# Attention's steps two by two in an order given to TensorE, beside the first feed-forward

## The chip, the cores and the metric

The program runs on one core of a Trainium2 chip. The metric is the device time of one execution in microseconds (us). The engines that matter are TensorE (PE, matrix multiplication, with its weight loads shown apart as PEld), VectorE (DVE), ScalarE (ACT), GpSimd (POOL), and SyncE (SP), which issues most of the DMAs. Each engine works through its own instructions in the order in which they stand in the program, and waits where a result of another engine is missing.

## The reference

Three layers follow each other. Attention has 4 batches of 8 heads, 576 positions and 64 columns to a head; its result is mixed with a read of a memory. Two feed-forward layers with 2304 tokens, 512 columns and 2048 hidden columns follow.

```python
scores = scale * np.matmul(q, k.transpose(0, 1, 3, 2))     # causal mask, softmax
local = np.matmul(a, v)
mem_ret = np.einsum('bhsd,bhde->bhse', q_p, M_prev)        # q_p = phi(q)
mem_out = mem_ret / mem_norm
attn = g * mem_out + (1 - g) * local
h = x @ w_in;  g = h * np.cos(h);            x = g @ w_out  # first feed-forward
h = x @ w_in;  g = h * np.tanh(softplus(h)); y = g @ w_out  # second feed-forward
```

## The kernel before

**Attention.** Two heads go together as a pair, 16 pairs in all. The queries of a pair are cut into five pieces, i = 0 to 4, of 128 positions; the last has 64 positions, and its two heads share one piece. One (pair, piece) is a step, so there are 80 steps, numbered from 0. A step has three stages, all in `attention`:

- Stage a (L240) multiplies queries with keys into PSUM (`sp`, L253: one matmul for each head with 64 contraction rows, so that the two heads use the upper and the lower half of the array; L266 for the last piece, with all 128 rows). VectorE adds the mask and finds the row's extreme (L255, L268), ScalarE takes the exponential and its sum (L258, L273), VectorE the reciprocal (L278), and GpSimd scales the rows (`at`, L280). With piece 0 the memory's read of the pair is made (`memory`, L284: `mp`, L293).
- Stage b (L304) transposes the rows `at` on TensorE, 128 columns at a time (`tp`, L313; `td`, L319, for the last 64 keys), and ScalarE and VectorE copy them to SBUF in turn (`aT`, `aD`).
- Stage c (L324) adds in one PSUM tile `o` the memory's share (L329, a matmul with the identity over all 128 output rows) and, for each 128 keys, the product with V of each head (L340, 64 output rows each, so that the two heads use the left and the right half of the array; the last 64 keys with 64 contraction rows too). ScalarE and VectorE then split the result into `xH` and `xL`, and SyncE stores them.

The text calls a matmul that uses the whole array full shape, the one of L253 half rows, the one of L340 half columns. Every float32 matmul of attention other than a transposition stands in the profile as two passes. The two heads of a half-row or half-column pair run at the same time when they stand next to each other.

**First feed-forward.** It runs over blocks of 256 tokens. One unit of `first` (L416) makes 24 matmuls into `h` (L429), and one unit of `second` (L436) makes 24 into `y` (L495). The cosine between them (`elem_cos`, L374) uses ScalarE (`u`, L383, and the sine, L388, with a table load before it and another one before the next exponential), VectorE and GpSimd (`g`, L401). A block of tokens can begin when its batch has left attention.

**What sets the order.** The loop at L354 issues for each s the stages c of step s-4, b of s-2 and a of s (LAGC, LAGB). The driver (L873 to L895) takes each yield: on "a" it issues conversions of weights, on "c" as many units of the first feed-forward as a target allows (L890 to L895). A scheduler in the framework then places the instructions on each engine by its own estimate of time, so feed-forward matmuls are put between those of attention wherever that estimate has room. `tc.issue_after(x)` adds only an order: the instructions in its block stand behind x on x's engine.

Of the kernel before, what the change touches and what calls it, by code (L numbers as in the profile page):

```python
# [23 lines left out]
RES = 2  # L24
# [10 lines left out]
PACE1 = 1.5  # L35
# [16 lines left out]
def attention_moe_moe_kernel(  # L52
# [140 lines left out]
    def attention(ap, pools):  # L193
# [46 lines left out]
        def stage_a(b, p, i):  # L240
            if i == 0:
                memory(b, p)
# [5 lines left out]
            if i < 4:  # L248
                N = P * (i + 1)
                sps = [bank("S", [P, SM], "sp") for _ in range(2)]  # L250
                for j, sp in enumerate(sps):
                    rows = slice(j * D, (j + 1) * D)
                    nc.tensor.matmul(sp[:, :N], st["q"][rows, q0:q0 + P], st["k"][rows, :N], start=True, stop=True)  # L253
# [7 lines left out]
            else:  # L261
                N = S
                at = ats[0]
                for k0, k1, w, name in ((0, SM, SM, "sp"), (SM, S, D, "sd")):
                    out = bank("S", [P, SM], name)
                    nc.tensor.matmul(out[:, :w], st["q"][:, q0:q0 + P], st["k"][:, k0:k1], start=True, stop=True)  # L266
# [17 lines left out]
        def memory(b, p):  # L284
# [3 lines left out]
            for c0, c1 in ((0, 3), (3, NQ)):  # L288
                nb = c1 - c0
                mp = bank("T", [P, nb, P + 2], "mp")  # L290
                for c in range(c0, c1):
                    q0 = min(c * P, S - P)
                    nc.tensor.matmul(mp[:, c - c0], st["ph"][:, q0:q0 + P], st["mz"], start=True, stop=True)  # L293
# [10 lines left out]
        def stage_b(b, p, i):  # L304
# [3 lines left out]
            for at in st["at", i]:  # L308
# [15 lines left out]
        def stage_c(b, p, i):  # L324
# [4 lines left out]
            nc.tensor.matmul(o[:, :n], st["mo"][:, i], ident[:, P - n:], start=True, stop=False,  # L329
                             skip_group_check=True)  # L330
            for c in range(i + 1):
                kk = P if c < 4 else D
                for j in range(2):
                    if i < 4:
# [17 lines left out]
        ns = len(steps)  # L352
        prep(*pairs[0])
        for s in range(ns + LAGC):  # L354
            if 0 <= s - LAGC < ns:
                stage_c(*steps[s - LAGC])
                yield "c", s - LAGC
            if 0 <= s - LAGB < ns:
                stage_b(*steps[s - LAGB])
                yield "b", s - LAGB  # L360
            if s < ns:
                b, p, i = steps[s]
                if i == PREP:
                    nx = s // NQ + 1
                    if nx < len(pairs):
                        prep(*pairs[nx])
                stage_a(b, p, i)
                yield "a", s
# [638 lines left out]
```

## Time and profile before

| | |
|---|---|
| median of 3 runs | 1042.88 us (1040.84 to 1043.91) |
| profiled execution | 1043.82 us, its span 1042.0 us |
| PE busy | 1006.5 us (97%), 6704 matmuls |
| DVE / POOL / ACT busy | 681.8 / 618.5 / 576.6 us |
| mean granted TensorE clock | 0.99 |
| chain that ended last | PE 65%, DVE 9%, DMA 8%, POOL 7%, issue 6% |

A row of the timeline gives the start, how long it lasted, engine, line, operation, the tiles (out<-in), the shape and how many instructions are merged. Matmuls overlap: the time that a group takes from the others is from its start to the start of the next row, not its own length. Attention's last matmul starts at 383.9 us, and the first matmul of the first feed-forward at 119.5 us; between those two both layers share TensorE.

### The profile page before, as it was taken

To read this page: it belongs to the slowest core of one execution; us is meant where nothing else is said; L and a number is where in the kernel's file an instruction comes from. 1 tells how busy PE (TensorE), PEld (TensorE's weight loads), DVE (VectorE), ACT (ScalarE), POOL (GpSimd) and SP (SyncE) were. 2 spreads that over 40 slices of the span, in tenths; PEclk is the share of its full clock that TensorE was granted. 3 is DMA by queue.
4 is the path that set the end of the run, shared out by engine and by line. 5 is a ranking of instruction groups with operands and counts; after the bars stand their busy time and mean duration, and the time that the engine had idled before them with its cause. 6 is when DMAs were issued, how large, how long until landed. Compare 5 with 4: busy or idle time off the path is not lost.

```text
span 1042.0 us, 19347 instructions
## 1 busy us (share of the span) xinstructions
PE 1006.5 (97%) x6704; PEld 895.9 (86%) x6704; DVE 681.8 (65%) x1423; ACT 576.6 (55%) x1274; POOL 618.5 (59%) x600
## 2 busy tenths in 40 slices
PE   6988999999999999999999999999999999999996
PEld 3755787787878899998788887899999999999996
DVE  4689865657665545777756776258787447862557
ACT  5886676758575643334546565347554545445441
POOL 3379744455553524665755776246877768786661
PEclk8998999999999999999999999999999999999999
DMA  7477734556442337433678777998988888798772
GB/s 268 143 237 237 224 112 161 184 177 213 138 148 82 139 106 261 154 108 126 223 269 280 281 291 289 399 311 291 385 295 272 273 284 288 244 297 267 262 239 107
DMA packets 121841, 236.19 MB, mean 227 GB/s; under 512 B 11920, under 2 KB 35984, under 8 KB 121744
## 3 DMA queue, kind: packets, MB, share of 16 engines
q1 hardware_dynamic: 117136, 220.27, 62.8%
q10 hardware_dynamic: 4608, 14.68, 3.5%
q8 instruction: 54, 0.88, 0.3%
q14 instruction: 43, 0.35, 0.1%
HBM read 176.44 MB, written 58.46 MB: 225 GB/s over the span
## 4 chain that ended last, share of the span: by engine, by line
PE 65%; DVE 9%; DMA 8%; POOL 7%; issue 6%; ACT 4%; SPq 1%; DVEq 0%; ACTq 0%; POOLq 0%
PE h L779 14%; PE y L750 13%; PE h L429 12%; PE y L495 11%; PE o L340 5%; PE tp L313 3%; PE sp L253 3%; PE o L329 2%; DVE wst L148 1%; DMA woD<-ws 1%; DVE wst L147 1%; POOL g L401 1%; DMA w<-woD 1%; PE mp L293 1%; DMA wst<-in_w1o_dram 1%
## 5 line engine op out<-in xcount | busy, mean ns | idle before, releaser
L684 POOL TENSOR_TENSOR g<-us,g 128x384 fp32r<-128x384 f32 x164 | 182.5, 1129 | 92.9 <-ACT g L131 92.7
L495 PE MATMUL y<-g,w 128*128 128x256 f32 (+1 forms) x1344 | 221.8, 318 | 3.2 <-ACT aT L131 1.6
L495 PEld LDWEIGHTS y<-g,w 128*128 128x128 f32 x1344 | 191.6, 190 | 30.7 <-issue 10.5
L429 PE MATMUL h<-xbH,w 128*128 128x256 f32 (+1 forms) x896 | 206.1, 317 | 1.4 <-DMA xbH<-xsH 1.3
L750 PE MATMUL y<-g,w 128*128 128x384 f32 x1008 | 194.7, 335 | 2.0 <-POOL g L684 1.4
L779 PE MATMUL h<-xc,wq 128*128 128x384 f32 x1008 | 194.8, 335 | 0.9 <-DVE us L673 0.9
L750 PEld LDWEIGHTS y<-g,w 128*128 128x128 f32 x1008 | 176.0, 188 | 4.1 <-POOL g L684 2.3
L401 POOL TENSOR_TENSOR g<-u,g 128x512 fp32r<-128x512 f32 x72 | 105.9, 1485 | 122.3 <-ACT g L131 40.1
L779 PEld LDWEIGHTS h<-xc,wq 128*128 128x128 f32 x1008 | 176.1, 188 | 1.2 <-DVE us L673 1.2
L280 POOL TENSOR_SCALAR at<-at,sm,omg 128x128 f32<-128x128 f32 (+2 forms) x144 | 112.9, 793 | 104.6 <-DVE sm L278 86.3
L429 PEld LDWEIGHTS h<-xbH,w 128*128 128x128 f32 x896 | 151.1, 191 | 14.0 <-DMA xbH<-xsH 1.8
L429 PE MATMUL h<-xbL,w 128*128 128x256 f32 (+1 forms) x448 | 140.8, 315 | 0.6 <-DMA xbL<-xsL 0.6
L673 DVE TENSOR_TENSOR us<-h,us 128x384 f32<-128x384 f32 x120 | 66.2, 553 | 91.2 <-PE h L779 76.2
L131 ACT ACTIVATE g<-us 128x384 fp32r<-128x384 f32 x168 | 85.7, 523 | 52.7 <-DVE us L668 28.5
L383 ACT ACTIVATE u<-h 128x512 int32<-128x512 f32 x72 | 42.8, 594 | 95.9 <-PE h L429 85.5
L429 PEld LDWEIGHTS h<-xbL,w 128*128 128x128 f32 x448 | 85.6, 191 | 6.2 <-DMA xbL<-xsL 1.1
L677 ACT ACTIVATE us<-us 128x384 f32<-128x384 f32 x72 | 37.7, 525 | 91.8 <-DVE us L673 86.7
L258 ACT ACTIVATE at<-at,mn 128x128 f32<-128x128 f32 (+3 forms) x128 | 71.1, 557 | 26.9 <-DVE mn L255 24.4
L384 DVE SCALAR_TENSOR_TENSOR u<-u,h 128x512 f32<-128x512 int32 x72 | 48.9, 681 | 47.5 <-ACT u L383 44.5
L148 DVE SCALAR_TENSOR_TENSOR wst<-wst 128x512 int32<-128x512 int32 x64 | 75.4, 1187 | 0.4
L714 DVE TENSOR_TENSOR ac<-y,ac 128x384 f32<-128x384 f32 x120 | 63.8, 550 | 18.0 <-PE y L750 17.1
L340 PE MATMUL o<-aT,vt 128*64 128x128 f32 (+1 forms) x896 | 67.3, 275 | 2.6 <-ACT aT L131 2.6
(109 smaller groups left out, 1519.7 us busy)
## 6 DMA issues: line engine op xcount, KB each, us to landing
wq<-wsD SPq DMA_DIRECT2D x168, 256.0 KB, 4.5
w<-woD SPq DMA_DIRECT2D x168, 256.0 KB, 4.5
wsD<-ws SPq DMA_DIRECT2D x18, 512.0 KB, 3.5
woD<-ws ACTq DMA_DIRECT2D x18, 512.0 KB, 5.3
wst<-in_w1i_dram SPq DMA_DIRECT2D x16, 512.0 KB, 4.1
wst<-in_w1o_dram SPq DMA_DIRECT2D x16, 512.0 KB, 4.6
wst<-in_w2i_dram SPq DMA_DIRECT2D x16, 512.0 KB, 4.2
wst<-in_w2o_dram SPq DMA_DIRECT2D x16, 512.0 KB, 5.4
```

Source lines behind the costliest of these rows:

```text
L131: eng.activation(dst, src, AF.Copy, scale=scale)
L148: nc.vector.scalar_tensor_tensor(lo, hi, 3, lo, ALU.logical_shift_left, ALU.bitwise_or)
L258: marks["act"] = nc.scalar.activation(at[:, :N], at[:, :N], AF.Exp, bias=mn[:, j:j + 1], scale=-1.0, accum_out=sm[:, j:j + 1]).ins
L280: marks["pool"] = turn_of("sc", b == 0).tensor_scalar(at[:, :N], at[:, :N], sm[:, j:j + 1], gates[j], ALU.mult, ALU.mult).ins
L340: marks["pe"] = nc.tensor.matmul(o[j * D:(j + 1) * D, :n], st["vt"][:kk, c, j * D:(j + 1) * D], a, start=False, stop=c == i, skip_group_ch ...
L401: marks["gl"] = turn_of(kind).tensor_tensor(gL, g, gH.bitcast(F32), ALU.subtract).ins
L429: nc.tensor.matmul(h[:, a * T:(a + 1) * T], w_[:, c, f0:f0 + P], x_[c], start=m == 0, stop=m == 3 * NC - 1)
L495: nc.tensor.matmul(y[e // per][:, cols], w_[:, f, es], g_, start=fst and m == 0 and e % per == 0, stop=lst and m == 2, skip_group_check=True)
L673: marks['v'] = nc.vector.tensor_tensor(c, b, x, ALU.add).ins
L684: ins = turn_of("ml" if k + 1 < n else "mz").tensor_tensor(t[:, 1], x, t[:, 0].bitcast(F32), ALU.subtract).ins
L750: nc.tensor.matmul(y, w_[:, wl, c], x[:, xl], start=m == 0, stop=m == 3 * KS - 1, skip_group_check=True)
L779: nc.tensor.matmul(b, w[name][:, wl, c], x[name][:, xl, c], start=first and m == 0, stop=m == 5, skip_group_check=True)
```

## The change

From step 30 on (PAIRS) the loop goes two steps at a time. Each stage of the two steps is issued behind the last matmul issued so far (`marks["pe"]`), so TensorE's order is given: the stages c that are due, then one or two units of the first feed-forward (PACE), then the memory's read, the stages b, and the stages a, the longer of the two first. Stage b lags a by one turn for the even step and by two for the odd one. The memory's share becomes two matmuls of 64 output rows. The last 64 keys of V are laid into the lower half of 128 rows, the upper half zero, and the transposition of the last keys takes 128 columns of `at`; so the last product has 128 contraction rows.

```diff
-RES = 2
-PACE1 = 1.5
+PAIRS = 30
+PACE = (1, 2, 2, 1, 2)
...
                 for c in range(0, W, P):
-                    nc.tensor.transpose(tp[:, c:c + P], at[:, c:c + P], ident)
+                    marks["pe"] = nc.tensor.transpose(tp[:, c:c + P], at[:, c:c + P], ident).ins
...
-                aD = ap.tile([P, 2, D], F32, tag="aD", name="aD", bufs=BUFS["aD"])
+                aD = ap.tile([P, P], F32, tag="aD", name="aD", bufs=BUFS["aD"])
                 tp = bank("T", [P, SM], "td")
-                nc.tensor.transpose(tp[:D, :P], at[:, SM:], ident)
-                scaled("aD", aD.rearrange("p a b -> p (a b)")[:D, :P], tp[:D, :P])
+                marks["pe"] = nc.tensor.transpose(tp[:, :P], at[:, S - P:], ident).ins
+                scaled("aD", aD, tp[:, :P])
...
-            nc.tensor.matmul(o[:, :n], st["mo"][:, i], ident[:, P - n:], start=True, stop=False,
-                             skip_group_check=True)
+            for j in range(2):
+                rows = slice(j * D, (j + 1) * D)
+                nc.tensor.matmul(o[rows, :n], st["mo"][:, i, rows], ident[:, P - n:], start=True, stop=False,
+                                 skip_group_check=True)
...
-                        a = st["aT", i][1][:D, j]
+                        a = st["aT", i][1][:, rows]
                     marks["pe"] = nc.tensor.matmul(
-                        o[j * D:(j + 1) * D, :n], st["vt"][:kk, c, j * D:(j + 1) * D], a,
+                        o[rows, :n], st["vt"][:, c, rows], a,
                         start=False, stop=c == i, skip_group_check=True).ins
...
+        def run(stage, ss):
+            for s in ss:
+                if 0 <= s < ns:
+                    with tc.issue_after(marks["pe"]):
+                        stage(*steps[s])
...
+        for s in range(PAIRS, ns + LAGC + 1, 2):
+            both = (s, s + 1)
+            run(stage_c, upto(s - LAGC + 1, 0))
+            yield "c", s - LAGC
+            for k in both:
+                coming(k)
+            run(banked, both)
+            run(stage_b, upto(s - LAGB + 1, 1))
+            run(stage_a, sorted(both, key=lambda k: -(k < ns and steps[k][2])))
+            for k in both:
+                if k < ns:
+                    yield "a", k
...
-        share = (r + 1) / steps_b
-        tgt = int(2 * NTL * (b - 1 + (share ** PACE1 if b == 1 else share))) - RES
-        while k_done < tgt:
-            converted(4 * min(k_done + 2, NTL))
-            _, kk = next(m1)
-            k_done = max(k_done, kk + 1)
+        stored[0] = (s + 1) // steps_b
+        for _ in range(PACE[s // 2 % NQ] if s >= PAIRS - LAGC else 0):
+            converted(4 * min(k_done // 4 * 2 + 3, NTL))
+            with tc.issue_after(marks["pe"]):
+                next(m1)
+            k_done += 1
...
     def rows(x):
         t = np.zeros((B, H, NQ * 128, D), x.dtype)
-        t[:, :, :S] = x
+        t[:, :, :S - D] = x[:, :, :S - D]
+        t[:, :, S:] = x[:, :, S - D:]
```

Before, TensorE's order puts the scores of one step, head by head, between matmuls of the feed-forward. L253 is the score matmul, L313 the transposition and L495 the feed-forward's `y`:

```order
L313 MATMUL tp<-ident,at 128x128 x4
L253 MATMUL sp<-kd,qd 128x512
L495 MATMUL y<-g,w_100 128x256 x2
L495 MATMUL y<-g,w_101 128x256
L495 MATMUL y<-g,w_100 128x256 x2
L253 MATMUL sp<-kd,qd 128x512
L495 MATMUL y<-g,w_101 128x256
```

The two heads' scores are five feed-forward matmuls apart, each with a change of shape before and behind it.

Now the order of the two steps 48 and 49 stands as follows, from the end of a feed-forward unit (h, L461) to the start of the next (y, L527). L314 is the transposition, L265 and L251 are the scores of the last piece and of the others, L332 the memory's share and L343 the product with V:

```order
L461 MATMUL h_2841<-xbH_1521,w011_95 128x256
L314 MATMUL tp_2893<-ident_73,at_2617 128x128
L314 MATMUL tp_2897<-ident_73,at_2618 128x128
L314 MATMUL tp_2901<-ident_73,at_2759 128x128 x2
L314 MATMUL tp_2906<-ident_73,at_2760 128x128 x2
L265 MATMUL sp_2914<-kd_2425,qd_2427 128x512
L265 MATMUL sd_2917<-kd_2425,qd_2427 128x64
L251 MATMUL sp_2928<-kd_2425,qd_2427 128x512
L251 MATMUL sp_2929<-kd_2425,qd_2427 128x512
L332 MATMUL o_2948<-ident_73,mo_2564 64x128 x2
L343 MATMUL o_2948<-aT_2894,vt_2431 64x128
```

The scores of both steps and the products with V now stand together, without feed-forward matmuls between them; 24 `y` matmuls, the memory's read and six transpositions follow, and then `tp_3016`, the transposition of the rows whose scores are `sp_2928`.

On ScalarE the piece of the order before one of the copies that stage c needs (`aT_2591`, of step 42; L415 and L420 are the feed-forward's `u` and its sine, L232 and L233 prepare the queries of a later pair) is now:

```order
L415 ACTIVATE u_2422<-h_2524 128x512
L347 ACTIVATE xH_2162<-o_2517 128x128
L232 ACTIVATE ph_3170<-qt_3168 128x576
L131 ACTIVATE aT_2581<-tp_2580 128x256
L420 ACT_TABLE_LOAD
L420 ACTIVATE u_2422<-u_2422,c_hpi_80 128x1024
L233 ACT_TABLE_LOAD
L233 ACTIVATE ph_3170<-ph_3170 128x576
L131 ACTIVATE aT_2591<-tp_2590 128x384
```

TensorE's matmuls behind `tp_2590` and `tp_2596` are the scores of steps 44 and 45 and then stage c of steps 41 and 42, whose last part begins with `aT_2591`; no feed-forward unit stands between.

## Rows read from the trace of the kernel before

**Rows 1.** Two stretches of 26 us: busy time of each engine, granted clock, DMA
```profile
core 0: us, PE busy (x) PEld busy (x) DVE busy (x) ACT busy (x) POOL busy (x), PEclk, DMA share, GB/s
104.00:130.00 26.00, 24.18 (x208) 18.68 (x208) 22.66 (x72) 18.06 (x58) 18.84 (x22) 0.93 0.69 221
...
260.00:286.00 26.00, 26.00 (x226) 22.73 (x227) 15.82 (x47) 14.21 (x42) 14.04 (x16) 1.00 0.42 137
```

**Rows 2.** Chain that ended last, 380 to 500 us: start, length, what
```profile
383.23 0.88 PE o L340 x20
...
391.61 5.76 PE h L429 x48
```

**Rows 3.** Timeline of PE, 268 to 280 us: start, length, engine, line, tiles, count
```profile
268.89 0.39 PE L329 MATMUL o<-ident,mo 128*128 128x128 f32 x2
269.21 0.88 PE L340 MATMUL o<-aT,vt 128*64 128x128 f32 x12
270.01 0.39 PE L429 MATMUL h<-xbH,w 128*128 128x256 f32 x1
270.24 0.28 PE L429 MATMUL h<-xbL,w 128*128 128x256 f32 x1
...
272.98 0.60 PE L313 MATMUL tp<-ident,at 128*128 128x128 f32 x4
273.41 0.27 PE L319 MATMUL td<-ident,at 128*64 128x128 f32 x1
273.61 0.70 PE L253 MATMUL sp<-kd,qd 64*128 64x256 f32 x4
274.25 0.49 PE L329 MATMUL o<-ident,mo 128*128 128x128 f32 x2
274.66 1.10 PE L340 MATMUL o<-aT,vt 128*64 128x128 f32 x16
275.69 0.74 PE L495 MATMUL y<-g,w 128*128 128x256 f32 x4
...
277.77 0.91 PE L253 MATMUL sp<-kd,qd 64*128 64x384 f32 x2
278.61 0.38 PE L495 MATMUL y<-g,w 128*128 128x256 f32 x1
```

**Rows 4.** Timeline of PE: three pauses, in brackets with what ended them
```profile
100.61 0.80 PE L329 MATMUL o<-ident,mo 128*128 128x128 f32 x2 [3.70 <-DVE mo L298]
...
117.09 0.49 PE L329 MATMUL o<-ident,mo 128*128 128x128 f32 x2 [1.82 <-DVE mn L255]
...
316.90 0.50 PE L495 MATMUL y<-g,w 128*128 128x256 f32 x2 [1.63 <-ACT aT L131]
```

**Rows 5.** Stretches behind the last two pauses, columns as in rows 1
```profile
117.60:120.90 3.30, 3.30 (x23) 2.97 (x24) 3.30 (x13) 1.73 (x7) 3.08 (x4) 0.50 0.52 158
...
318.70:322.10 3.40, 3.40 (x31) 3.40 (x30) 1.53 (x4) 2.58 (x9) 3.06 (x4) 1.00 0.34 130
```

**Rows 6.** Timeline of PE, from a feed-forward unit's end to the scores of step 48
```profile
201.41 0.60 PE L313 MATMUL tp<-ident,at 128*128 128x128 f32 x4
201.94 1.13 PE L253 MATMUL sp<-kd,qd 64*128 64x512 f32 x4
203.00 0.49 PE L329 MATMUL o<-ident,mo 128*128 128x128 f32 x2
```

**Rows 7.** Timeline of ACT, the same stretch
```profile
201.61 0.60 ACT L383 ACTIVATE u<-h 128x512 int32<-128x512 f32 x1 [1.44 <-PE h L429]
...
202.51 1.28 ACT L388 ACT_TABLE_LOAD   x1
203.80 1.15 ACT L388 ACTIVATE u<-u,c_hpi 128x1024 f32<-128x1024 f32 x1
...
206.26 0.72 ACT L258 ACTIVATE at<-at,mn 128x512 f32<-128x512 f32 x1
...
208.36 0.47 ACT L131 ACTIVATE aT<-tp 128x384 f32<-128x384 f32 x1
```

**Rows 8.** Timeline of POOL, the rows of step 48 scaled
```profile
211.01 1.51 POOL L280 TENSOR_SCALAR at<-at,sm,omg 128x512 f32<-128x512 f32 x2
```

**Rows 9.** Timeline of SP's queue: the first blocks' loads
```profile
89.31 1.00 SPq L482 DMA_DIRECT2D xbH<-xsH  x2
...
93.17 2.04 SPq L482 DMA_DIRECT2D xbL<-xsL  x2
```

**Rows 10.** Timeline of PE: step 27's stage c, the first feed-forward's first matmul
```profile
111.69 0.39 PE L329 MATMUL o<-ident,mo 128*128 128x128 f32 x2
...
119.53 0.56 PE L429 MATMUL h<-xbH,w 128*128 128x256 f32 x1
```

More of the change, by code (lines that the diff above doesn't have):

```diff
@@ L252, in stage_a @@
                     rows = slice(j * D, (j + 1) * D)
-                    nc.tensor.matmul(sp[:, :N], st["q"][rows, q0:q0 + P], st["k"][rows, :N], start=True, stop=True)
+                    marks["pe"] = nc.tensor.matmul(sp[:, :N], st["q"][rows, q0:q0 + P], st["k"][rows, :N],
+                                                   start=True, stop=True).ins
                 for j, (at, sp) in enumerate(zip(ats, sps)):
@@ L265, in stage_a @@
                     out = bank("S", [P, SM], name)
-                    nc.tensor.matmul(out[:, :w], st["q"][:, q0:q0 + P], st["k"][:, k0:k1], start=True, stop=True)
+                    marks["pe"] = nc.tensor.matmul(out[:, :w], st["q"][:, q0:q0 + P], st["k"][:, k0:k1],
+                                                   start=True, stop=True).ins
                     if k0 == 0:
@@ L292, in memory @@
                     q0 = min(c * P, S - P)
-                    nc.tensor.matmul(mp[:, c - c0], st["ph"][:, q0:q0 + P], st["mz"], start=True, stop=True)
+                    marks["pe"] = nc.tensor.matmul(mp[:, c - c0], st["ph"][:, q0:q0 + P], st["mz"],
+                                                   start=True, stop=True).ins
                 den = ap.tile([P, nb, 2], F32, tag="den", name="den", bufs=BUFS["den"])
@@ L352, in attention, with coming, banked, upto @@
         ns = len(steps)
+        def coming(s):
+            if s < ns and steps[s][2] == PREP and s // NQ + 1 < len(pairs):
+                prep(*pairs[s // NQ + 1])
+        def run(stage, ss):
[3 more added lines that the diff above has]
+                        stage(*steps[s])
+        def banked(b, p, i):
+            if i == 0:
+                memory(b, p)
         prep(*pairs[0])
-        for s in range(ns + LAGC):
-            if 0 <= s - LAGC < ns:
+        for s in range(PAIRS):
+            if s >= LAGC:
                 stage_c(*steps[s - LAGC])
                 yield "c", s - LAGC
-            if 0 <= s - LAGB < ns:
+            if s >= LAGB:
                 stage_b(*steps[s - LAGB])
[L360 to L368, printed above, removed]
+            coming(s)
+            banked(*steps[s])
+            stage_a(*steps[s])
+            yield "a", s
+        done = [PAIRS - LAGC, PAIRS - LAGB]
+        def upto(n, k):
+            out = range(done[k], n)
+            done[k] = n
+            return out
+        for s in range(PAIRS, ns + LAGC + 1, 2):
[10 more added lines that the diff above has]
+                    yield "a", k
     last_sin = [None]
@@ L494, in mm2_t @@
             for m, (w_, g_) in enumerate(((woH, gH), (woH, gL), (woL, gH))):
-                nc.tensor.matmul(y[e // per][:, cols], w_[:, f, es], g_, start=fst and m == 0 and e % per == 0,
-                                 stop=lst and m == 2, skip_group_check=True)
+                marks["pe"] = nc.tensor.matmul(y[e // per][:, cols], w_[:, f, es], g_,
+                                               start=fst and m == 0 and e % per == 0,
+                                               stop=lst and m == 2, skip_group_check=True).ins
     def part(ys_, blk, i):
```

13 lines of the change are left out of this document (3 added, 10 removed).

## The prediction

> **What bounds the kernel now.** I read the page's shares first, then the chain of waits, then a table by stretches, then TensorE's own timeline, and last the timelines of ScalarE and GpSimd at the places where TensorE will have to wait for them. The shares show TensorE busy for 97% of the span, and the chain gives it 65%. The table by stretches [rows 1] shows how this comes about inside attention: from 260 us TensorE is busy for the whole 26 us while VectorE, ScalarE and GpSimd stand at 14 to 16 us; from 104 us it has 24.18 of 26 us, with VectorE at 22.66 close behind. So behind step 23's stage c (100.61 us, behind the last long pause of the early part) TensorE's own work and its pauses set the pace, up to attention's last matmuls, which begin at 383.23 us and end at 384.1 [rows 2]. What follows is dense: 48 matmuls of the feed-forward in 5.76 us [rows 2], 0.12 us each, and nothing of the change lies there. What the change is worth is therefore TensorE's time saved between 100.6 and 384.1 us, less new pauses, and less what the clock takes.
>
> **Split heads.** I went along TensorE's order from stage c of step 23 to the end of the first feed-forward, before and after. Before, in ten steps the scores of the two heads stand apart (four of 384 columns, three of 512, two of 128, one of 256); after, in none. What standing apart costs is in TensorE's timeline [rows 3]: one head alone with 384 columns takes 0.84 us (277.77 to 278.61). Two heads with 256 columns take 0.64 (273.61 to 274.25), and two with 512 take 1.06 (201.94 to 203.00) [rows 6]. By these two, 384 columns for both would be between 0.64 and 1.06, 0.85, what one head alone takes. So a head alone costs as much as the pair, and each split step pays its pair's time once too often: 4 x 0.84 + 3 x 1.06 + 0.64 + 2 x 0.42 (an estimate, half of 0.84) = 7.9 us, about 8.0.
>
> **Changes of shape.** Along the same way the order has 213 changes between full, half-row and half-column shapes before and 88 after, 125 fewer. The price comes from TensorE's timeline [rows 3]. Full to half columns and back: the two passes of L329 take 0.32 (268.89 to 269.21) ahead of a change where two transpositions take 0.22, 0.10 more; the 12 passes of L340 take 0.80 where six pairs at 0.115 (the 16 passes at 274.66 take 1.03, so two more pairs 0.23) make 0.69, 0.11 more, or 0.14 by pairs at 0.11; the first h behind them takes 0.23 where a dense one takes 0.12, 0.11 more. Together 0.32 to 0.35; I take 0.35. Half rows: td, ahead of the change, takes 0.20 instead of 0.11, 0.09 more, and L329 between half rows and half columns (274.25 to 274.66) takes 0.41 instead of 0.32, again 0.09; I take 0.19 for both and the rounding. So one change costs 0.175 or 0.095. Between 125 x 0.095 = 11.9 and 125 x 0.175 = 21.9 us I take the middle, 16.9. The memory's share is no longer a full matmul: two half-column matmuls side by side cost a pair's two passes, 0.23, against 0.22, so nothing but the change of shape is saved, and that is counted.
>
> **V's last keys.** The last product has 128 instead of 64 contraction rows at the same columns, and the transposition td 128 instead of 64 output rows. The timeline [rows 3] has four transpositions from 272.98 to 273.41, 0.11 each, and td from 273.41 to 273.61, 0.20 with the change to half rows behind it. I put nothing for either, bounded by 0.1 us a last piece (ten of them, 1 us) both ways. The Trainium skill (TensorEngine Tiling (Array Packing), Key Properties) says that a change of tiling mode drains TensorE, and td with its 64 output rows would be such a change, in and out; by that rule ten of them at 0.135 twice would give 2.7 us more. The 0.43 us of the four rows ahead of td show no drain, so the trace does not bear it out there.
>
> So TensorE's work falls by 8.0 + 16.9 = 25 us, 20 to 30 by the bounds.
>
> **New pauses.** Before, matmuls of the feed-forward go wherever a step waits. Now the order is given, and the work behind a wait can't step ahead. I take two places of the ten steps after which pieces and PACE repeat; attention has five such tens from step 30.
>
> The first is the transposition tp_3016, which waits for the scaled rows of step 48. Before, from the unit's end (201.41) [rows 6] the path of scores, minimum, exponential [rows 7], scaling [rows 8] needed until 211.77 for the first head (211.01 and half of 1.51): 10.36 us; for the second 11.1. After, TensorE has between the two events: six transpositions 0.66, the scores of both steps 2.2 (1.06 for step 48, for the whole rows of step 49's piece an estimate of as much), ten pairs of half columns 1.15 with 0.24 for the changes, 24 y at 0.12 with a change 3.0, the memory's ten passes 1.1, six more transpositions 0.66; 9.0 us. The pause is 10.36 - 9.0 = 1.35 for the first head; the second head's rows come 0.74 later but are wanted only 0.44 later (four transpositions), 0.3 more: 1.65. It is 2.4 if one more exponential (0.72) [rows 7] stands ahead, since step 49's scores now go first. I take 2.0.
>
> The second is stage c of step 42, whose aT_2591 now stands on ScalarE behind u, a table load, the sine, another load and the two ph. Before, from the start of u to the first exponential behind the sine it took 4.65 (201.61 to 206.26), and a copy 0.47 [rows 7]. With two activations of the exponential's size for ph, 1.44, and 0.2 to the start of u, aT is there 6.8 us behind the start. TensorE has in that time the memory's read 1.1, transpositions 1.1, scores 1.06 and 0.93, changes and the first pairs 0.6; 4.8 us. Pause: 2.0.
>
> With some 1.1 us in small pauses a ten (from none, where the other wait is late enough, to twice that), this makes 5.1 us, five times 25.5. Bounds: 12.8, where half of each wait is covered by work that I counted as late, and 35. What goes are two pauses of before [rows 4], 1.82 (VectorE's minimum) and 1.63 (ScalarE's copy): 3.5 us. The pause of 3.70 lies ahead of the change.
>
> **The clock.** Behind the pause of 1.82 the granted clock was 0.50 for 3.3 us, 1.2 instead of 2.4 GHz; behind that of 1.63 it stayed at 1.00 [rows 5]. A fall costs half of its 3.4 us, 1.7. Ten pauses of about 2.0 come, one of two such was followed by a fall; since the fall stands in the stretch with the idler TensorE, 0.93 granted against 1.00 [rows 1], I take four of ten. One of before goes: 3 x 1.7 = 5.1 us more. Bounds: -1.7 and 9 x 1.7 = 15.3.
>
> **The sum** is made on the profiled execution, 1043.82 us (span 1042.0, the rest before and behind it unchanged): -25 + 25.5 - 3.5 + 5.1 = +2.1, so 1045.9. The profiled execution lies 0.9 above the median of the three runs; against the median the forecast is 1045.0. Little is changed for other queues: SP's and POOL's instructions keep nearly their sequence. The first unit comes right behind stage c of step 27, which before begins at 111.69 us, so some 7 us earlier than its 119.53 [rows 10]; its loads are issued from 89 to 95 us [rows 9], ahead of that. Were they late there, the unit would wait for what its earlier start gains and no more. With 44 units inside attention instead of 40, fewer dense matmuls follow; that is in the 25 us, as the count goes to the end of the first feed-forward.
>
> **Rivals.** *The clock falls behind every long pause, and TensorE is slower than before.* Mechanism: tp_3016 waits on GpSimd and aT_2591 on ScalarE at every ten, and half speed follows each time; ten falls at 1.7 in place of the one of before, 15.3 instead of 5.1, so +12.3: 1055. For it: every idle time in the order is a true one now. Against it: the pause of 1.63. It decides from the seventh fall on.
>
> *The waits are mostly covered.* The path of 10.36 us was measured where VectorE and ScalarE worked between other steps; if the new order brings the exponential and the scaling forward by 1 us, both pauses halve: 12.8 us, and with none followed by a fall, -25 + 12.8 - 3.5 - 1.7 = -17.4: 1025.5. For it: outside the stretch from 104 us the three engines have over 10 of 26 us idle [rows 1]. Against it: the order is strict.
>
> *VectorE becomes the bound from 104 us.* It is busy for 22.66 of 26 us [rows 1]; going 9% faster (25 of 283 us) it would be at 24.7, so any bunching makes it late, and a fifth of the 25 us, 5.0, is lost there: 1050.
>
> *A table load holds ScalarE for longer where a copy stands right behind it.* If each of the two loads ahead of aT_2591 held ScalarE for twice its 1.29 us (202.51 to 203.80) [rows 7], in five tens 2 x 1.29 x 5 = 12.9 us come on top: 1057.9. Against it: the sine starts right at the load's end, and the second load is already in the 4.65 us. The Trainium skill (ScalarE: Activation LUTs, What ACT_TABLE_LOAD costs) would have it so: about 1283 ns for the load and a drain of about 1380 ns, 2.66 us in all; the row of 1.29 shows the load and no drain.
>
> **How the numbers follow.** This kernel's measurement tells 0.3%, 3.1 us, from no change: 1039.8 to 1046.0. My forecast has 0.42 with its own range from 1037 to 1052 (shape changes 5 either way, pauses as much); 0.55 of it lies within 0.3%, a quarter below, a fifth above. The covered waits have 0.30, the clock 0.22, VectorE 0.03, the loads 0.03. Faster: 0.30 + 0.11 = 0.41. Same: 0.23. Slower: 0.22 + 0.03 + 0.03 + 0.08 = 0.36. The range goes from 1023 to 1058.
>
> **What would show it.** Each step right: scores of both heads as one row of four passes throughout; half-column rows that begin with the memory's share; pauses of about 2 us in TensorE's timeline at stage b, ended by GpSimd's scaling, and at stage c, ended by ScalarE's aT, two in ten steps; stretches at half clock behind some of them; the second feed-forward's first matmul some 2 us later than before. The forecast is wrong if the sum of TensorE's pauses in attention is under 13 us or over 35, if the clock never falls behind 104 us or falls at every ten, or if a pair of heads side by side takes more than here.

## The result and the profile after

The changed kernel takes 1058.48 us (median of 4 runs, 1056.42 to 1060.03) against 1043.39 us before; the ratio is 1.0146 with an interval of 1.0124 to 1.0169. It is slower, by 15 us where 2 were forecast, and lies half a microsecond above the upper end of the range. The profiled execution has a span of 1058.2 us, 16.2 more than before.

The page of the changed kernel, busy time by engine and the chain's shares:

```profile
span 1058.2 us, 19552 instructions
...
PE 997.1 (94%) x6864; PEld 897.7 (85%) x6864; DVE 683.2 (65%) x1423; ACT 578.1 (55%) x1276; POOL 617.9 (58%) x600
...
PE 54%; POOL 12%; DVE 11%; issue 8%; ACT 8%; DMA 5%; SPq 0%; ACTq 0%; DVEq 0%; POOLq 0%
```

TensorE was busy 97% of the time and is now at 94%; the chain passes from it to GpSimd, ScalarE and VectorE, so it waits for them. Where the time went is shown by two stretches of each kernel, the first from stage c of step 23 to the second half of the first feed-forward (its first matmul with 512 columns), the second from there to the end (columns as in [rows 1]). Before:

```profile
100.60:472.10 371.50, 366.88 (x3066) 316.47 (x3067) 240.75 (x642) 218.98 (x515) 185.55 (x200) 0.99 0.48 159
472.10:1042.00 569.90, 556.89 (x3026) 521.96 (x3024) 370.17 (x535) 280.38 (x528) 371.46 (x320) 1.00 0.79 272
```

After:

```profile
100.10:481.00 380.90, 354.28 (x3183) 317.35 (x3182) 239.09 (x642) 221.93 (x522) 186.92 (x199) 0.96 0.45 155
481.00:1058.20 577.20, 557.96 (x3026) 523.81 (x3024) 376.90 (x541) 282.01 (x531) 375.67 (x325) 0.99 0.78 270
```

The first stretch is 9.4 us longer, the second 7.3, though nothing of the change lies in the second. In the first, the mean granted clock falls from 0.99 to 0.96.

TensorE's pauses in the first stretch (its timeline; in brackets the pause and what ended it) are where the prediction had put them:

```profile
169.66 0.66 PE L314 MATMUL tp<-ident,at 128*128 128x128 f32 x4 [1.78 <-POOL at L280]
171.58 0.63 PE L314 MATMUL tp<-ident,at 128*128 128x128 f32 x4 [1.27 <-POOL sw L595]
...
196.58 0.44 PE L332 MATMUL o<-ident,mo 128*64 128x128 f32 x4 [1.79 <-ACT aT L131]
...
225.28 0.66 PE L314 MATMUL tp<-ident,at 128*128 128x128 f32 x4 [1.79 <-POOL at L280]
226.48 0.63 PE L314 MATMUL tp<-ident,at 128*128 128x128 f32 x4 [0.55 <-DVE mo L299]
227.04 1.65 PE L251 MATMUL sp<-kd,qd 64*128 64x256 f32 x8
...
306.62 0.44 PE L332 MATMUL o<-ident,mo 128*64 128x128 f32 x4 [1.84 <-ACT aT L131]
```

225.28 is tp_3016, the transposition of step 48, with 1.79 us where 2.0 were taken; 196.58 is stage c of step 42, 1.79 where 2.0 were taken. ScalarE's timeline ahead of it shows the chain that was forecast: the copy aT that ends the pause is done 6.8 us behind the start of u.

```profile
189.77 0.58 ACT L415 ACTIVATE u<-h 128x512 int32<-128x512 f32 x1
...
193.01 1.15 ACT L420 ACTIVATE u<-u,c_hpi 128x1024 f32<-128x1024 f32 x1
194.17 1.28 ACT L233 ACT_TABLE_LOAD   x1
195.47 0.68 ACT L233 ACTIVATE ph<-ph 128x576 f32<-128x576 f32 x1
196.06 0.47 ACT L131 ACTIVATE aT<-tp 128x384 f32<-128x384 f32 x1
```

Against [rows 4] there are 18 pauses of over 0.25 us with 25.0 us in all, before 4 with 4.6.

In this execution the clock falls behind pauses at stage b and not behind those at stage c (stretches of the changed kernel, columns as in [rows 1]):

```profile
172.50:175.50 3.00, 3.00 (x26) 2.64 (x24) 1.73 (x9) 2.00 (x8) 0.00 (x0) 0.50 0.35 98
227.00:230.00 3.00, 3.00 (x24) 2.56 (x24) 1.80 (x9) 1.66 (x6) 0.00 (x0) 0.50 0.83 263
282.00:285.00 3.00, 3.00 (x18) 2.27 (x19) 2.17 (x9) 1.04 (x3) 0.59 (x1) 0.50 0.24 73
336.50:342.50 6.00, 6.00 (x44) 5.27 (x46) 1.76 (x10) 3.86 (x13) 0.19 (x1) 0.50 0.16 61
...
197.00:200.00 3.00, 3.00 (x34) 2.83 (x29) 1.45 (x8) 2.00 (x8) 2.32 (x2) 1.00 1.00 358
307.00:310.00 3.00, 3.00 (x33) 2.83 (x30) 1.48 (x8) 1.97 (x8) 2.29 (x2) 1.00 1.00 344
```

The column behind POOL's is the clock. Seven stretches at 0.50 lie in this part of the execution, six of 3.4 us and one of 6.8, against one of 3.4 before and the end of another. From 172 us on there is one in every ten steps, at stage b of steps 38, 48, 58, 68 and 78 (172, 227, 282, 336 and 391 us).

The second stretch has one pause that was not there. In the changed kernel's timeline of TensorE:

```profile
504.92 0.79 PE L461 MATMUL h<-xbH,w 128*128 128x512 f32 x1 [7.05 <-DVE u L423]
```

Of ScalarE, in the time before:

```profile
492.48 0.59 ACT L415 ACTIVATE u<-h 128x512 int32<-128x512 f32 x1
501.56 0.65 ACT L131 ACTIVATE wst<-wst 128x512 f32<-128x512 f32 x1 [8.49 <-DMA wst<-in_w2i_dram]
502.12 0.63 ACT L146 ACTIVATE wst<-wst 128x512 int32<-128x512 uint32 x1
502.66 1.13 ACT L420 ACTIVATE u<-u,c_hpi 128x1024 f32<-128x1024 f32 x1
```

And of SP's queue:

```profile
494.00 0.39 SPq L139 DMA_DIRECT2D wst<-in_w2i_dram  x1
```

Before, ScalarE had:

```profile
492.62 1.15 ACT L388 ACTIVATE u<-u,c_hpi 128x1024 f32<-128x1024 f32 x1
...
494.24 0.66 ACT L131 ACTIVATE wst<-wst 128x512 f32<-128x512 f32 x1
```

and SP's queue:

```profile
479.88 0.39 SPq L139 DMA_DIRECT2D wst<-in_w2i_dram  x1
```

Now ScalarE's conversion of a piece of weights stands ahead of the sine and waits 8.49 us for its load, which SP issues at 494.00; the sine and TensorE's next matmul wait with it, and the clock is at 0.50 for 10.2 us, from 500.0 to 510.3. Before, the load went out at 479.88, and the piece stood behind the sine.

### The profile page after: what moved, and what is told of

It is laid out like the page before. It is cut to its first block, busy times and chain, and to the rows that moved or that the text cites. A ratio compares the mean times of both kernels' runs of the same rounds, so it can differ in the third digit from the quotient of the medians.

```text
span 1058.2 us, 19552 instructions
## 1 busy us (share of the span) xinstructions
PE 997.1 (94%) x6864; PEld 897.7 (85%) x6864; DVE 683.2 (65%) x1423; ACT 578.1 (55%) x1276; POOL 617.9 (58%) x600
## 4 chain that ended last, share of the span: by engine, by line
PE 54%; POOL 12%; DVE 11%; issue 8%; ACT 8%; DMA 5%; SPq 0%; ACTq 0%; DVEq 0%; POOLq 0%
PE h L812 15%; PE y L783 15%; PE h L461 7%; PE y L527 5%; POOL g L433 3%; PE o L343 3%; PE sp L251 3%; PE tp L314 3%; POOL sw L595 2%; DVE wst L148 2%; POOL at L280 2%; POOL ws L601 2%; ACT at L257 1%; PE o L332 1%; ACT u L420 1%
## 5 line engine op out<-in xcount | busy, mean ns | idle before, releaser
L717 POOL TENSOR_TENSOR g<-us,g 128x384 fp32r<-128x384 f32 x164 | 185.9, 1152 | 95.4 <-ACT g L131 87.4
L527 PE MATMUL y<-g,w 128*128 128x256 f32 (+1 forms) x1344 | 214.4, 315 | 0.0
L461 PE MATMUL h<-xbH,w 128*128 128x256 f32 (+1 forms) x896 | 205.0, 317 | 8.0 <-DVE u L423 7.6
L527 PEld LDWEIGHTS y<-g,w 128*128 128x128 f32 x1344 | 189.7, 190 | 17.9 <-issue 2.2
L280 POOL TENSOR_SCALAR at<-at,sm,omg 128x128 f32<-128x128 f32 (+4 forms) x144 | 116.1, 817 | 117.7 <-DVE sm L278 101.3
L433 POOL TENSOR_TENSOR g<-u,g 128x512 fp32r<-128x512 f32 x72 | 103.7, 1457 | 121.4 <-DVE g L133 56.8
L461 PEld LDWEIGHTS h<-xbH,w 128*128 128x128 f32 x896 | 151.0, 192 | 20.9 <-DVE u L423 8.2
L461 PE MATMUL h<-xbL,w 128*128 128x256 f32 (+1 forms) x448 | 141.3, 316 | 0.3 <-DMA xbL<-xsL 0.3
L461 PEld LDWEIGHTS h<-xbL,w 128*128 128x128 f32 x448 | 85.9, 192 | 6.0 <-DMA xbL<-xsL 0.8
L415 ACT ACTIVATE u<-h 128x512 int32<-128x512 f32 x72 | 42.4, 594 | 82.1 <-PE h L461 66.0
L314 PE MATMUL tp<-ident,at 128*128 128x128 f32 x384 | 64.0, 295 | 24.6 <-POOL at L280 14.5
L314 PEld LDWEIGHTS tp<-ident,at 128*128 128x128 f32 x384 | 45.0, 148 | 39.0 <-POOL at L280 31.7
```

The costliest lines, as they stand in the source:

```text
L280: marks["pool"] = turn_of("sc", b == 0).tensor_scalar(at[:, :N], at[:, :N], sm[:, j:j + 1], gates[j], ALU.mult, ALU.mult).ins
L314: marks["pe"] = nc.tensor.transpose(tp[:, c:c + P], at[:, c:c + P], ident).ins
L433: marks["gl"] = turn_of(kind).tensor_tensor(gL, g, gH.bitcast(F32), ALU.subtract).ins
L461: marks["pe"] = nc.tensor.matmul(h[:, a * T:(a + 1) * T], w_[:, c, f0:f0 + P], x_[c], start=m == 0, stop=m == 3 * NC - 1).ins
L527: marks["pe"] = nc.tensor.matmul(y[e // per][:, cols], w_[:, f, es], g_, start=fst and m == 0 and e % per == 0, stop=lst and m == 2, skip_ ...
L717: ins = turn_of("ml" if k + 1 < n else "mz").tensor_tensor(t[:, 1], x, t[:, 0].bitcast(F32), ALU.subtract).ins
```

## The experiments

Each row below is read from the profiled execution: the length of the first stretch (stage c of step 23 to the first matmul with 512 columns), the pauses of over 0.25 us in it, what half clock cost (half of the time at 0.50), the rest, called TensorE's work, and the second stretch. The rest holds shorter waits too. The median is that of all runs; the profiled execution lies 2.4 us below it in the third experiment, 4.5 below in the tenth and 3.0 above in the eleventh.

| kernel | median us | first stretch | pauses | half clock | work | second stretch |
|---|---|---|---|---|---|---|
| before | 1043.39 | 371.5 | 4.6 | 3.4 | 363.5 | 569.9 |
| after | 1058.48 | 380.9 | 25.0 | 13.7 | 342.2 | 577.2 |
| 1 shapes alone | 1035.46 | 364.5 | 4.6 | 1.7 | 358.2 | 567.6 |
| 2 order alone | 1064.88 | 384.5 | 21.1 | 10.2 | 353.2 | 577.7 |
| 3 two more pieces | 1050.02 | 374.0 | 27.6 | 3.4 | 343.0 | 569.1 |
| 4 even step first | 1053.35 | 373.7 | 16.9 | 8.5 | 348.3 | 576.5 |
| 5 V's rows alone | 1042.43 | 369.8 | 4.7 | 3.3 | 361.8 | 568.2 |
| 6 units first | 1068.96 | 389.8 | 31.7 | 10.2 | 347.9 | 578.1 |
| 7 units first, 3 and 4 | 1051.04 | 379.4 | 20.6 | 8.5 | 350.3 | 569.9 |
| 8 3 and 4 | 1040.95 | 372.1 | 17.1 | 6.8 | 348.2 | 567.6 |
| 9 filled | 1054.81 | 373.5 | 17.5 | 1.7 | 354.3 | 578.0 |
| 10 other pace | 1051.76 | 378.0 | 25.1 | 8.5 | 344.4 | 569.0 |
| 11 aT on VectorE | 1053.42 | 385.1 | 21.3 | 15.4 | 348.4 | 568.9 |
| 12 filled and 3 | 1050.10 | 376.6 | 19.7 | 3.4 | 353.5 | 571.0 |

**1. The shapes' edits alone**, in the kernel before.

```diff
-            nc.tensor.matmul(o[:, :n], st["mo"][:, i], ident[:, P - n:], ...)
+            for j in range(2):
+                nc.tensor.matmul(o[rows, :n], st["mo"][:, i, rows], ident[:, P - n:], ...)
...
-                nc.tensor.transpose(tp[:D, :P], at[:, SM:], ident)
+                nc.tensor.transpose(tp[:, :P], at[:, S - P:], ident)
```

> The kernel before with its own order of work, but with the memory's share as two half-column matmuls, V's last keys as 128 rows and td over 128 columns. Theory A (those edits are harmless, the order is what costs): 1037 to 1044 us, no pause at the second half's weights, no more than one fall of the clock behind 104 us. Theory B (the shapes themselves cost, a pair of half-column matmuls being dearer than one full matmul): slower than 1046.

Measured: 1035.46 us, ratio 0.9912 (0.9884 to 0.9940). Theory B is out, and Theory A was too low on the gain: the edits that I had costed at nothing but changes of shape make the kernel before 8 us faster. Along TensorE's order 186 changes are left of 213. The scheduler also puts many matmuls of this stretch in another order than before, so the gain is that of the edits together with the order that follows from them.

**2. The order alone**: the changed kernel with the three edits of the first experiment taken back.

> The changed kernel's order of work, but the memory's share as one full-shape matmul, V's last keys as 64 rows and td as before. Theory A: 1056 to 1064 us, with the same pauses at stage b, a half-speed stretch behind each of them, and the 7 us pause near 505 us. Theory B: under 1052.

Measured: 1064.88 us, ratio 1.0202 (1.0168 to 1.0235), just above the expectation's upper end. The loss belongs to the given order. Its first stretch has 21.1 us of pauses, half clock at five places, and the late sine returns with a pause of 8.41 us. One part of the expectation missed: the clock doesn't fall behind each pause at stage b (there is none behind 2.58 us at 284.18), and two of the five falls stand behind pauses at stage c. One of these pauses in TensorE's timeline, and the stretch behind it with the clock at 0.50:

```profile
197.30 0.49 PE L330 MATMUL o<-ident,mo 128*128 128x128 f32 x2 [2.12 <-ACT aT L131]
...
197.90:201.20 3.30, 3.30 (x22) 2.97 (x21) 1.35 (x6) 2.00 (x8) 2.53 (x2) 0.50 1.04 382
```

With some 180 changes and no split heads, TensorE's work is still 10.3 us less than before. The changed kernel has almost the same order of matmuls, so the two together give the worth of the edits in a given order: 6.4 us of time (1064.88 to 1058.48), and 11.0 us of TensorE's work for some 90 changes fewer, 0.12 each.

**3. Two more pieces of weights** beside the rest of the first feed-forward.

```diff
-            if i % 2 == 0:
+            if i % 2 == 0 or i in (1, 3):
                 with tc.issue_after(marks["cos"]), tc.issue_after(last_sin[0]):
                     done_b = next(gb, done_b)
```

> The changed kernel, but two more pieces of the second half's weights are fetched and converted beside the rest of the first feed-forward behind attention, so that as many are done before the second half begins as in the kernel before (16 for 32 remaining yields, now 14 for 28). Theory A (44 instead of 40 yields inside attention leave fewer behind it, and the conversion of weights is tied to those): the pause of 7.05 us near 505 us and the half speed behind it go, 1048 to 1051 us. Theory B (the pause comes from a slow transfer of that execution or of another cause): 1056 or more.

Measured: 1050.02 us (10 runs, 1046.73 to 1057.2), ratio 1.0064 (1.0039 to 1.0090). The load of w2 goes out at 483.55, 6.95 us behind the stretch's start (7.78 before, 13.0 after), the 7 us pause is gone, and the second stretch is 569.1 us, as before. Theory A is shown. The surprise is in the first stretch, where TensorE's order is that of the changed kernel. Its timeline at the transposition of step 48:

```profile
226.33 0.66 PE L314 MATMUL tp<-ident,at 128*128 128x128 f32 x4 [1.77 <-POOL at L280]
227.53 0.63 PE L314 MATMUL tp<-ident,at 128*128 128x128 f32 x4 [0.54 <-DVE mo L299]
228.09 0.92 PE L251 MATMUL sp<-kd,qd 64*128 64x256 f32 x8
```

There are the same pauses, 1.77 and 0.54, but the eight score matmuls behind them take 0.92 us, where those of the changed kernel take 1.65 (227.04 above). TensorE's matmuls of the first stretch are the same in the same order. In this execution the clock falls twice there, not seven times. So a pause of this size makes a fall possible and does not decide it. The mean clock of the ten runs goes from 0.970 to 0.986 and the time the other way: the two runs at 0.970 and 0.971 take 1054.98 and 1057.20, the one at 0.986 takes 1046.73.

**4. The even step's scores first.**

```diff
-            run(stage_a, sorted(both, key=lambda k: -(k < ns and steps[k][2])))
+            run(stage_a, both)
```

> The changed kernel, but of the two steps of a turn the even one's scores go first, whose rows are wanted one turn later (the odd one's two turns later). Theory A (the clock falls where a pause at stage b and those next to it add up to over 2 us): the pauses at stage b ended by GpSimd are 0.7 to 2 us shorter each, at most three falls behind 104 us remain, 1043 to 1051 us. Theory C (the place decides, since transpositions and scores follow at stage b, not the length): the pauses get shorter, the falls stay at seven or so, 1050 to 1056. If the scaling isn't brought forward at all: 1057 or more.

Measured: 1053.35 us. The step whose rows are wanted a turn earlier is now first in every queue, and the pause at tp_3016 shrinks from 1.79 to 0.47 us in TensorE's timeline:

```profile
224.11 0.66 PE L314 MATMUL tp<-ident,at 128*128 128x128 f32 x4 [0.47 <-POOL at L280]
```

All pauses together: 16.9 instead of 25.0 us. The clock falls five times behind step 23, where three were expected at most. One fall (171.9 us) lies 3.9 us behind a pause of only 0.41, but between them the eight score matmuls take 2.35 us at full clock, where the third experiment's took 0.92:

```profile
169.28 2.35 PE L251 MATMUL sp<-kd,qd 64*128 64x128 f32 x8
```

So there are waits that the sum of pauses doesn't count. They show in the table too: TensorE's work, with the same matmuls, is 348.3 us instead of 342.2, which takes back 6 of the 8 us that the pauses lose.

Three falls now follow stage c; two of its pauses are 2.28 us instead of 1.79 and 1.84. The first in TensorE's timeline:

```profile
195.24 0.44 PE L332 MATMUL o<-ident,mo 128*64 128x128 f32 x4 [2.28 <-ACT aT L131]
```

The stretch behind it, with the clock at 0.50:

```profile
196.00:199.00 3.00, 3.00 (x19) 2.67 (x16) 1.19 (x6) 2.21 (x8) 2.54 (x2) 0.50 0.98 336
```

That stage b is the place where the clock falls (Theory C) is out.

**5. V's last keys alone**, without the memory's share.

> The kernel before with V's last keys as 128 rows and td over 128 columns, but the memory's share as one full-shape matmul as before. Along TensorE's order 201 changes of shape instead of 213 (186 in the first experiment, with the memory's share in halves too). Theory D (what the shapes' edits gain is the changes of shape, 0.15 to 0.27 us each): 1040 to 1042.5 us, most of the 8 us belongs to the memory's share. Theory E (the gain lies in the last keys, whose 64-row matmuls drain TensorE twice): 1035 to 1038.

Measured: 1042.43 us (10 runs), ratio 0.9985 (0.9972 to 0.9998). About 1 us, as Theory D has it, near the 12 changes of shape that it saves. TensorE's order of matmuls is that of before. The other 7 us of the first experiment come with the memory's share as two half columns, and with the order that the scheduler makes of it.

**6. Units ahead of stage c.**

```diff
-            run(stage_c, upto(s - LAGC + 1, 0))
-            yield "c", s - LAGC
+            yield "u", s - LAGC
+            run(stage_c, upto(s - LAGC + 1, 0))
```

> The changed kernel, but the one or two feed-forward units of a turn stand ahead of its stage c instead of behind it (the tiles aT are made as wide as their content, so that memory suffices). Theory A: between a step's transpositions and its products with V now lie the scores and a unit of 2.9 us or two, so the pauses at stage c ended by ScalarE's aT (1.79, 0.76 with 1.21, 1.85, 0.45 us) go, about 8 us less; 25 more changes of shape cost about 4 us; the pauses at stage b stay, with falls of the clock behind some: 1050 to 1057 us. Theory F (the wait only moves on to stage b): 1059 or more.

Measured: 1068.96 us, ratio 1.0239 (1.0218 to 1.0260): Theory F. The pauses at stage c are gone, but others came, at stage b and a new one ahead of the scores (TensorE's timeline):

```profile
275.73 1.12 PE L265 MATMUL sp<-kd,qd 128*128 128x512 f32 x2 [1.27 <-ACT aT L131]
...
287.14 1.41 PE L314 MATMUL tp<-ident,at 128*128 128x128 f32 x8 [2.79 <-POOL at L280]
```

The new pause is 1.27 us five times over, as long as a table load (1.28 in [rows 7]): I read it as a place in PSUM that is now freed by a copy behind such a load on ScalarE. That reading was not tested. In this order a unit moved to one wait is missing at the next.

**7. All three edits** (units first, even step first, two more pieces).

> The changed kernel with all three edits: units ahead of stage c, the even step's scores first, and two more pieces of weights converted beside the rest of the first feed-forward. Theory A: pauses at stage b and c together under 8 us instead of 25, at most two falls of the clock behind 104 us, no pause near 505 us, 25 more changes of shape: 1030 to 1040 us, faster than before. If the pauses come back elsewhere (VectorE or ScalarE late as a whole): 1044 or more.

Measured: 1051.04 us, ratio 1.0064 (1.0045 to 1.0084). A miss: 20.6 us of pauses remain, among them the new one of 1.27 us.

**8. Even step first and two more pieces**, without the units' move.

> The changed kernel with the even step's scores first and two more pieces of weights, units behind stage c as in the changed kernel. Theory A: the gains of both add up, 5 us and 8 us: 1043 to 1048 us, with the pauses at stage c (1.2 to 2.3 us) left. Theory G (how often the clock falls is set anew in each execution and outweighs the pauses): a spread of over 5 us between its runs, as in the third experiment.

Measured: 1040.95 us (10 runs, 1038.13 to 1042.27), ratio 0.9972 (0.9959 to 0.9984): 0.3% faster than before, 2 us better than the expectation. The two edits together are worth 17.5 us against the changed kernel. The spread is 4 us, so Theory G is not borne out here. 17.1 us of pauses and four falls are left, all four behind stage c, as this row of TensorE's timeline:

```profile
192.88 0.70 PE L332 MATMUL o<-ident,mo 128*64 128x128 f32 x4 [2.21 <-ACT aT L131]
```

**9. Filled.** Ahead of stage b of steps 38, 48, 58, 68 and 78 the changed kernel transposes the identity 16 times into the tile that the step overwrites.

```diff
+                if fill and at is st["at", i][0]:
+                    for _ in range(16):
+                        marks["pe"] = nc.tensor.transpose(tp[:, :P], ident, ident).ins
```

> The changed kernel, with 16 transpositions of the identity (1.76 us) ahead of the transpositions of steps 38, 48, 58, 68 and 78, where the changed kernel pauses for 1.8 to 3.0 us at stage b and its clock falls behind every one of the five. They go into the tile that the true transpositions overwrite, so nothing else changes. Theory A (it is the idle TensorE ahead of it that lets the clock fall): the five falls at 172, 227, 281, 336 and 391 us go, about 8 us less: 1047 to 1053 us. Theory G (falls come wherever the execution happens to be, filled or not): five or more falls stay, 1056 to 1061 us. Theory H (the filling is in the way): more than 1061.

Measured: 1054.81 us, ratio 1.0112 (1.0087 to 1.0137). The falls at the five places are gone, the clock stays at 1.00 there (one fall is left in the first stretch, at 129.5 us), and the scores behind have their full pace, in TensorE's timeline:

```profile
223.57 1.91 PE L315 MATMUL tp<-ident 128*128 128x128 f32 x16
225.51 1.40 PE L317 MATMUL tp<-ident,at 128*128 128x128 f32 x8
226.84 0.92 PE L251 MATMUL sp<-kd,qd 64*128 64x256 f32 x8
```

Two of the stretches, with the clock behind POOL's column:

```profile
228.00:231.00 3.00, 2.82 (x42) 2.65 (x43) 1.23 (x9) 2.44 (x10) 0.00 (x0) 1.00 0.95 309
...
336.00:339.00 3.00, 3.00 (x42) 2.83 (x39) 0.58 (x7) 3.00 (x12) 0.00 (x0) 1.00 0.08 26
```

It is the idle TensorE that lets the clock fall, as Theory A says; half clock costs 1.7 instead of 13.7 us. Since the third experiment had only one fall at the five places without any filling, one execution would not show this. But the twelfth, filled too, has none there either, which makes none in ten, against eight in fifteen in the three given orders without filling (the changed kernel, the second and the third experiment); and the mean clock is 0.979 to 0.984 in all four runs, against 0.972 to 0.976 in those of the changed kernel. The time gains less than the 5 to 11 us that Theory A gave, since what fills takes 1.94 us a place (223.57 to 225.51), 9.7 in all, and the pauses shrink by 7.5 only.

**10. Another pace**, in the eighth experiment: 2, 2, 2, 1, 1 units.

> The eighth experiment (1040.95 us) with the units dealt out otherwise: 2, 2, 2, 1, 1 over the five turns, from the turn with pieces 0 and 1 on, and one fewer at first, so that no turn's units end with the second half of a pair of h, behind which u, the table loads and the sine stand ahead of aT on ScalarE. Theory A (that is what stage c waits for): the pauses of 2.2 and of 0.76 with 1.2 us at stage c are under 1 us; 1032 to 1038 us. If the shorter turns make stage b late instead: 1040 to 1047.

Measured: 1051.76 us, ratio 1.0069 (1.0042 to 1.0096). Both theories gave less. No pause at stage c over 0.94 us is left, as it should be if stage c waited for copies behind the sine; but some of the scores now wait for ScalarE's copies, up to 1.76 us, and stage b behind the turns with one unit now waits for up to 3.3 us, as in TensorE's timeline:

```profile
203.12 0.66 PE L314 MATMUL tp<-ident,at 128*128 128x128 f32 x4 [3.24 <-POOL at L280]
```

**11. Every copy aT on VectorE**, in the eighth experiment (`aT="v"` for `aT="av"`).

> The eighth experiment (1040.95 us) with every copy aT on VectorE instead of ScalarE and VectorE in turn. Theory A (stage c waits for the copies that stand behind the sine on ScalarE): the pauses at stage c go, 1032 to 1038 us. If VectorE is late itself with more to do: pauses ended by DVE aT of the same length, 1040 to 1048.

Measured: 1053.42 us, ratio 1.0087 (1.0056 to 1.0119), above both readings. The long pauses at stage c are gone here too (0.71 us at most), so it was ScalarE's copies that they waited for. Others come at stage b, 1.25 to 1.88 us behind 200 us, ended by GpSimd's scaling, while VectorE ahead of it is busier: 130.57 us from 200 to 400 us, in the eighth experiment 116.02. The pauses sum to 21.3 us, with 15.4 us of half clock.

**12. Filled, and two more pieces.**

> The changed kernel with both edits: 16 transpositions of the identity ahead of stage b of steps 38, 48, 58, 68 and 78, and two more pieces of weights converted beside the rest of the first feed-forward. Theory A (the prediction left out two things, the falls behind the pauses at stage b and the pause near 505 us): the two gains add up, 1043 to 1048 us, what the prediction gave for the changed kernel, with at most three falls behind 104 us and no pause over 2 us behind attention. If they share a cause, or the falls come back elsewhere: 1050 or more.

Measured: 1050.10 us, ratio 1.0065 (1.0040 to 1.0090), at the border of the two readings, and no faster than the third experiment. The falls at the five places and the pause behind attention are gone, as expected (two other falls are left), but the time that they would have taken is spent on filling; where the clock mostly holds anyway, filling gains nothing.

## Why the prediction was wrong

By its own steps, for the profiled executions:

| step | forecast | measured |
|---|---|---|
| TensorE's work | -25 | -21.3 |
| pauses, new less gone | +22.0 | +20.4 |
| half clock | +5.1 | +10.3 |
| up to step 23 | 0 | -0.5 |
| behind attention | 0 | +7.3 |
| sum | +2.1 | +16.2 |

**The work** was right within its bounds of 20 to 30. With split heads at 8.0 (the terms of that sum make 8.0, not the 7.9 that it states), 13.3 us are left for 125 changes of shape, 0.11 each where 0.135 were taken; split heads were not measured apart, but the 0.12 that the second experiment gives is near. One statement is open: "nothing but the change of shape is saved" by the memory's share. In the given order it agrees with the 0.12 for each change. In the old order the first and fifth experiment differ by 7 us, of which the work of the first stretch shows 3.6 (361.8 to 358.2) for 15 changes, twice the price; the rest is half clock (1.6) and the time outside the stretch. As the scheduler's order changed as well, the runs don't show how much of this is the shape.

**The pauses** were right in place and cause and near in size: 25.0 us, of which 22.6 stand behind step 30, where 25.5 were taken.

**Half clock** is the first step that failed, by size. The prediction took four falls in ten pauses from one fall behind two pauses [rows 5]. The changed kernel had seven in that stretch, one twice as long, so 10.3 us instead of 5.1. By the prediction's own signs that decides against it: its rival was to hold "from the seventh fall on", and the forecast was to be wrong if the clock "falls at every ten", which it does from 172 us on. The rival with a fall behind every long pause had the direction and, at 1055, nearly the time, but not quite the mechanism: the pauses at stage c had none. The third experiment shows that seven is not fixed either: two falls with the same pauses. What decides for one execution stays open: place does not (second and fourth experiment), and the pause's length alone does not (third).

**"Nothing of the change lies there"** is the second step that failed, and this one for its reason. The stretch behind attention was left out because its instructions are unchanged. But the conversion of the second half's weights is tied to the feed-forward's yields that remain: one piece for every two. With 44 instead of 40 yields inside attention, 28 remain instead of 32, and 14 pieces instead of 16 are done when the second half begins; the rest then comes ahead of the sine. I had counted the 44 yields as "fewer dense matmuls" and not asked what else hangs on them. The third experiment gives two more pieces and has the second stretch back at 569.1 us.

The range was missed by half a microsecond, so either step alone would have left the time inside it: the third experiment, without the pause behind attention, measures 1050.02 us, and with half clock as forecast the sum would be 5.2 us less. The other terms, 3.7 us less saved and 1.6 us less lost, would not have led out of it.

**The forecast's other signs**: the scores stand as pairs throughout, the half-column rows begin with the memory's share, two long pauses come in ten steps, and the falls stand behind some; the second half of the first feed-forward begins 8.9 us later than before. The second feed-forward's first matmul, for which some 2 us were forecast, comes 23.9 us later; before, twelve of its matmuls stood ahead of the first feed-forward's last block, now none does. The first rows of it in TensorE's timeline, before and after:

```profile
660.25 2.27 PE L779 MATMUL h<-xc,wq 128*128 128x384 f32 x12
...
684.17 2.60 PE L812 MATMUL h<-xc,wq 128*128 128x384 f32 x14
```

**The other rivals.** The waits are not mostly covered: the pauses sum to 25.0 us, not 12.8. A table load does not hold ScalarE for longer: the row of 194.17 above is followed by the next activation 1.30 us behind its start. That VectorE becomes the bound from 104 us does not show: it is busy for 22.98 of 26 us there, before for 22.66, and TensorE for 25.54, before for 24.18 [rows 1].

```profile
104.00:130.00 26.00, 25.54 (x244) 21.29 (x243) 22.98 (x62) 16.11 (x41) 18.21 (x20) 0.93 0.62 202
```

The fastest kernel of all is the first experiment, with the shapes' edits and the scheduler's free order: 1035.46 us. The given order alone (second experiment) saves more of TensorE's work than those edits, 10.3 us against 5.3, but spends it on waiting; with the even step first and two more pieces (eighth experiment) it comes to 1040.95.

## What to carry to other kernels

An order written out by hand removes what a free order uses to fill waits, so each wait in it must be covered by counted work, and work moved to one wait is missing at another; start the step first whose result is wanted first. Where work is moved to an earlier stage, look for everything that is dealt out by its count, such as loads and conversions tied to a loop's remaining turns. A small edit that saves changes of shape can be worth more than the new order that it came with, so time the parts apart. A sum of pauses counts only those above its threshold: when an edit shortens them, see whether the same matmuls now take longer between them.

## What the runs showed of the hardware

TensorE's granted clock, 1.00 or 0.50 (2.4 or 1.2 GHz), fell behind many pauses of 1.8 to 3.1 us, not behind others as long, and came back after 3.4 us, in one case of the changed kernel's attention after 6.8. With the same matmuls in the same order and nearly the same pauses it fell seven times in one execution and twice in another. Where transpositions of the identity filled the idle time, no fall came at any of the five places in either of two executions. Eight half-row score matmuls took 0.92 us at 1.00 and 1.65 us at 0.50. One change between full, half-row and half-column shapes cost about 0.12 us (an estimate), by the second experiment against the changed kernel. On ScalarE the activation behind a table load started 1.30 us behind the load's start.
